# Attention with memory and two feed-forward layers on one core: attention groups reordered, weights converted in place, the first two blocks taken in two sweeps

## The chip, the cores and the metric

One core of a Trainium2 chip. The metric is the device time of one execution in microseconds (us), the median of several runs.

## The reference

```python
# B, H, S, D = 4, 8, 576, 64; all inputs float32 or float64 as drawn
scores = scale * q @ k^T, causal, softmax      # local attention
local  = a @ v
q_p    = phi(q)                                # phi(x) = where(x > 0, x, exp(x) - 1) + 1
mem    = (q_p @ M_prev) / (q_p @ z_prev + 1e-6)
g      = sigmoid(beta) per head
x      = g * mem + (1 - g) * local             # 2304 tokens x 512
x      = leaky(x @ w_in, 0.01) @ w_out         # first layer, d_ff = 2048
y      = (h - tanh(h)) @ w2_out, h = x @ w2_in # second layer, d_ff = 2048
```

The weights come as float64 and are used to a precision above one float32r product: each is split into a high and a low part, and so is each activation.

## The kernel before

**Two phases.** In the first, attention and the first layer run side by side, and the weights of both layers are turned from float64 to float32. In the second (from line 975 on) the second layer runs alone, with an order written out by hand; the change does not touch it.

**Attention** is cut into 32 units: four batches, for each a group A (queries 0 to 255, keys 0 to 255) and a group B (queries 256 to 575, all keys), for each group four pairs of heads. `Unit.declare` (L405) lists a unit's work: loads (L423 to L454), phi of q and its denominators on ScalarE and VectorE (L465 to L499), scores on TensorE (L538), maximum, exponential and sum (L571 to L607), scaling of the exponentials by 1/sum and by 1 - g (`pscale`, L609), transposes (L645, L664), the value products (L683, L686) and the copy of the result to a tile `x` (`fin`, L699). There is one x tile for the A groups and one for the B groups (`xA`, `xB`). The last 64 queries of each B group go to a ninth block R by way of DRAM.

**The first layer** takes nine blocks of 256 tokens (`layer1`, L801): the eight groups in the order A0, B0, A1, B1, ..., and R. A block's x is split into a high and a low part (`x_hi`, `x_lo`, L817 to L829; one buffer `xs`), then eight steps p follow, one for each pair of 128-column tiles of the hidden width. A step p (here an *item*) is 24 up matmuls (L794), the leak, a copy to the high part `gh`, the subtraction for the low part `gl`, and 24 down matmuls (L878). The leak is a copy from PSUM on ScalarE (`leak_a`, L848, run by the helper at L372) and a VectorE operation (`leak_b`, L853). The sums stay in PSUM (`dn0`, `dn1`) over all eight steps and are then copied out and stored (L892 to L902).

**The weights**: `convert` (L714) loads a chunk of 256 columns of a tile as integer words into a ring of four `cvr`, makes float32 words of it in a ring of four `cv` (one ScalarE operation and four VectorE operations, L731 to L747), and for the first layer writes the high part (`w_hi`, L760) and the low part (`w_lo`, L763) to the weight tile. There are 64 chunks for each layer; those of the second layer are stored to DRAM and loaded again in phase two.

**The order of the work** on each engine comes from a planner, `Schedule.run` (L144). Every piece of work has its engines with an estimated duration on each, what it reads, writes and allocates, and a due time `prio`. The planner plays the program through: whenever an engine is free, it takes the ready piece with the smallest due time that has room in its rings (`room`, L130) and emits it. On the chip each engine then runs its pieces in this order. Attention units have due times 0 to 31 with small offsets (`OFFSET`, L220), conversions of the first layer `W1_FROM + i * W1_STEP` (L225, L914), those of the second layer come behind given units, and matmuls of the first layer have the due time class `MOE_PE`, so that TensorE takes them when attention has nothing ready. `BIAS` (L224) weighs the engines where a piece can go to several. All loads and stores are issued by SP.

```python
groups = [("A", 0), ("B", 0), ("A", 1), ("B", 1), ("A", 2), ("B", 2), ("A", 3), ("B", 3)]
BIAS = {"act": 1.25, "dve": 2.5, "pool": 0.9}
W1_FROM, W1_STEP = 0, 0.15
chunks = [(m, f, c) for p in range(NP) for m in range(2) for f in (2 * p, 2 * p + 1) for c in range(512 // CW)]
```

Of the kernel before, what the change touches and what calls it, by code (L numbers as in the profile page):

```python
# [19 lines left out]
TINY = 2.0 ** -15  # L20
# [38 lines left out]
def POOL(n):  # L59
    return 160 + 0.83 * n  # L60


def POOL_S(n):
    return 328 + 0.83 * n


def POOL_TT(n):
    return 165 + 2.07 * n
# [12 lines left out]
class Op:  # L81
    __slots__ = (
        "alts", "fn", "prio", "lat", "alloc", "deps", "users", "left", "tiles", "end", "engine", "idx")


class Schedule:
# [15 lines left out]
    def op(self, alts, fn, reads=(), writes=(), alloc=(), prio=(0,), lat=0.0, after=(), war=False, order=False):  # L102
        o = Op()
        o.alts, o.fn, o.prio, o.lat, o.alloc = dict(alts), fn, prio, lat, tuple(alloc)
# [39 lines left out]
    def run(self):  # L144
# [13 lines left out]
        cold = 0.0  # L158
        events = [1000.0]
        t = -1.0  # L160
        while todo:
# [6 lines left out]
            while again:  # L168
                again = False
                for e in engines:  # L170
                    if free[e] > t:
                        continue
                    for i, (_, _, at, o) in enumerate(ready[e]):
                        if at > t or not self.room(o, t):
                            continue
# [19 lines left out]
                    o.engine, o.end = e, mine  # L195
                    free[e] = mine
# [27 lines left out]
BIAS = {"act": 1.25, "dve": 2.5, "pool": 0.9}  # L224
W1_FROM, W1_STEP = 0, 0.15  # L225
# [4 lines left out]
def kernel(  # L230
# [42 lines left out]
    mask = const.tile([128, 640], BF16, name="mask")  # L273
# [9 lines left out]
    with tc.tile_pool(name="id0", bufs=1) as id_p:  # L283
# [10 lines left out]
        out=mask[:, 512:640], in_=mask[:, 512:640], pattern=[[-1, 128]], compare_op=ALU.is_ge,  # L294
        fill=-8.0e9, base=0, channel_multiplier=1,
    )
    nc.vector.tensor_copy(out=mask4[:, 0:512], in_=mask[:, 0:512])
    for i in range(2):
        nc.vector.tensor_copy(out=mask4[64 * i:64 * i + 64, 512:S], in_=mask[0:64, 512:S])
# [9 lines left out]
    nc.vector.tensor_scalar(out=omg, in0=gate, scalar1=-1.0, scalar2=1.0, op0=ALU.mult, op1=ALU.add)  # L309
    for i in range(2):  # L310
# [4 lines left out]
    wt = [[wts.tile([128, 1024], F32R, name=f"w{m}_{f}") for f in range(NF)] for m in range(2)]  # L315
# [4 lines left out]
    def w_load(raw, a, m, f, c):  # L320
        if m == 0:
            src = a[c * CW:(c + 1) * CW, f * 128:(f + 1) * 128].bitcast(I32)
            nc.sync.dma_start(
                out=raw.rearrange("p (k c) -> p k c", k=CW // 128),
                in_=src.rearrange("(k p) c -> p k c", p=128))
        else:
            nc.sync.dma_start(
                out=raw, in_=a[f * 128:(f + 1) * 128, c * CW:(c + 1) * CW].bitcast(I32))
# [5 lines left out]
    groups = [("A", 0), ("B", 0), ("A", 1), ("B", 1), ("A", 2), ("B", 2), ("A", 3), ("B", 3)]  # L334
# [12 lines left out]
    x2s = [dram.tile([128, KT, 256], F32, name=f"x2s{n}") for n in range(NBLK)]  # L347
    x8s = dram.tile([128, KT, 256], F32, name="x8s")
# [3 lines left out]
    x_p = p1.enter_context(tc.tile_pool(name="x", bufs=1))  # L352
# [12 lines left out]
    w_h = [[[sc.new(None) for _ in range(512 // CW)] for f in range(NF)] for m in range(2)]  # L365
    v_h = [[sc.new(None) for f in range(NF)] for m in range(2)]
    x8_h = sc.new(None)
    x2_h = [sc.new(None) for n in range(NBLK)]

# [20 lines left out]
    class Unit:  # L390
# [14 lines left out]
        def declare(self, pr, prev):  # L405
# [40 lines left out]
            def load_v(e):  # L446
                v_.tile = att.tile([128, 5, 2, 64], F32, name="v", bufs=RINGS["v"])
                for i, h in enumerate(heads):
                    nc.sync.dma_start(
                        out=v_.tile[:, 0:nk, i, :],  # L450
                        in_=v[b, h, 0:nk * 128, :].rearrange("(t p) d -> p t d", p=128))
# [12 lines left out]

            def phi_exp(e):  # L465
                ph.tile = att.tile([128, 3, 2, 64], F32, name="ph", bufs=RINGS["ph"])
                nc.scalar.activation(out=flat(ph.tile), in_=flat(rq.tile), func=AF.Exp)

            def phi_line(e):
# [3 lines left out]
            def phi_min(e):  # L473
                nc.vector.tensor_tensor(out=flat(ph.tile), in0=flat(ph.tile), in1=flat(rq.tile), op=ALU.min)
# [25 lines left out]
            op([("act", ACT(nf))], phi_exp, reads=[rq], alloc=[ph])  # L500
            op([("dve", DVE(nf / 2))], phi_line, reads=[rq], writes=[rq], war=True)
            op([("dve", DVE(nf))], phi_min, reads=[rq, ph], writes=[ph])
            op([("dve", 2 * nq * 145)], phi_den, reads=[ph, zb], writes=[rq], alloc=[dn])
            op([("dve", 110)], den_inv, reads=[dn], writes=[dn])
# [16 lines left out]
            op(copies(nqc, True), p_out, reads=[s], writes=[pT])  # L521
# [41 lines left out]
            for i in range(nq):  # L563
# [7 lines left out]
                def maxi(e, j, t=t, ss=ss, ei=ei, mx=mx, nn=nn, half=half, c0=c0):  # L571
                    if t < 4:
                        out, in0, in1 = ei.tile[:, j, :], ss[j].tile[:, c0:c0 + nn], mask[:, 640 - nn:640]
# [14 lines left out]
                for j in range(2):  # L588
                    op([("dve", DVE(width))], lambda e, j=j, f=maxi: f(e, j),
# [11 lines left out]
                def sum_eps(e, t=t, sm=sm):  # L601
                    x = sm.tile[:, 0:2 if t < 4 else 1]
                    nc.vector.tensor_scalar(out=x, in0=x, scalar1=1e-9, scalar2=None, op0=ALU.add)
# [5 lines left out]
                def pscale(e, j, t=t, ei=ei, sm=sm):  # L609
                    x = ei.tile[:, j, :] if t < 4 else ei.tile[:, 0:S]  # L610
                    g = omg[:, 2 * hp + j:2 * hp + j + 1] if t < 4 else omg4[:, hp:hp + 1]
                    (nc.vector if e == "dve" else nc.gpsimd).tensor_scalar(  # L612
                        out=x, in0=x, scalar1=sm.tile[:, j:j + 1], scalar2=g, op0=ALU.mult, op1=ALU.mult)
# [6 lines left out]
                op([("dve", 85)], sum_inv, reads=[sm], writes=[sm])  # L620
                for j in both:
                    op([("pool", POOL_S(nn)), ("dve", DVE(0.83 * nn))], lambda e, j=j, f=pscale: f(e, j),
# [13 lines left out]
            for kt in range(nk):  # L636
# [42 lines left out]
                for j in range(len(ss)):  # L679
                    op(copies(2 * w if len(ss) == 1 else w, True), lambda e, j=j, f=e_out: f(e, j),  # L680
                       reads=[ss[j]], writes=[pt])

            def pv(e):  # L683
                for kt, c0, w, pt, at in parts:
                    for j in range(2):
                        nc.tensor.matmul(  # L686
                            o.tile[64 * j:64 * j + 64, c0:c0 + w], lhsT=v_.tile[:, kt, j, :],
# [7 lines left out]
            if first_x:  # L695
                x_h[key] = new("x" + kind)
            xh = x_h[key]

            def fin(e):  # L699
                if xh.tile is None:  # L700
                    xh.tile = x_p.tile([128, KT, nqc], F32, name="x" + kind)
                copy(e, xh.tile[:, hp, 0:nqc], o.tile[:, 0:nqc])

            op(copies(nqc, True), fin, reads=[o], writes=[xh], alloc=[xh] if first_x else [])
# [9 lines left out]
    def convert(m, f, c, layer, pr, after=()):  # L714
        a = ((w1_in, w1_out), (w2_in, w2_out))[layer][m]
        raw, g = sc.new("cvr"), sc.new("cv")
        op = lambda *a, **kw: sc.op(*a, prio=pr, **kw)

        def load(e):
            raw.tile = cv_p.tile([128, 2 * CW], I32, name="cvr", bufs=RINGS["cvr"])  # L720
            w_load(raw.tile, a, m, f, c)
# [3 lines left out]

        def gi():
            return g.tile.bitcast(I32)

        def c_abs(e):
            g.tile = cv_p.tile([128, CW], F32, name="cv", bufs=RINGS["cv"])  # L730
            nc.scalar.activation(out=g.tile, in_=words(1).bitcast(F32), func=AF.Abs)  # L731

        def c_max(e):
            nc.vector.tensor_scalar(out=g.tile, in0=g.tile, scalar1=TINY, scalar2=None, op0=ALU.max)  # L734
# [17 lines left out]
        op([("act", ACT(CW))], c_abs, reads=[raw], alloc=[g])  # L752
        op([("dve", DVE(CW / 2))], c_max, reads=[g], writes=[g])
# [360 lines left out]
```

## Time and profile before

| | us |
|---|---|
| median of 3 runs | 1130.25 |
| lowest, highest | 1127.24, 1130.68 |
| the profiled execution | 1126.48 |
| its span, first to last instruction | 1124.8 |
| TensorE busy in the span | 1049.4 (93%) |
| VectorE busy | 750.9 (67%) |
| ScalarE busy | 584.1 (52%) |
| GpSimd busy | 422.0 (38%) |

PE is TensorE's matmuls, PEld its weight loads, which overlap them; DVE is VectorE, ACT ScalarE, POOL GpSimd, SP the engine that issues the transfers. L794 is line 794 of the kernel. Busy shares in slices are in tenths of the slice; PEclk is the granted clock of TensorE in tenths of full speed, or as a fraction in a table by stage. A busy DVE or POOL instruction can hold time in which it was kept waiting. The span lies 1.7 us under the execution's own time.

### The profile page before, as it was taken

How to read it: one execution, taken by the hardware profiler on the slowest of the kernel's cores; microseconds unless marked ns; L12 is line 12 of the kernel's file. 1: busy time of each engine (PE TensorE's matmuls, PEld its weight loads, DVE VectorE, ACT ScalarE, POOL GpSimd, SP SyncE). 2: the span in 40 equal slices, each digit the busy share in tenths (PEclk: the TensorE clock that was granted, in tenths of full speed). 3: DMA queues.
4: the chain of work that ended last, by engine and by line, in shares of the span. 5: the costliest groups of instructions: out<-in, count | busy, mean ns of one | idle time of the engine just before them, and what ended most of it. 6: DMA issues, size and time to landing. Idle time of an engine off the chain costs nothing.

```text
span 1124.8 us, 20884 instructions
## 1 busy us (share of the span) xinstructions
PE 1049.4 (93%) x7488; PEld 915.8 (81%) x7488; DVE 750.9 (67%) x2015; ACT 584.1 (52%) x1285; POOL 422.0 (38%) x462
## 2 busy tenths in 40 slices
PE   4468889999999999999999999899999999999997
PEld 2246677779688797797999999899999999999996
DVE  8999998676973956926111115577777777777774
ACT  4556555554643635515111122576666676676664
POOL 4556555334342343343333358622222222222221
PEclk8679999999999999999999999999999999999999
DMA  6545453444742744605110014501001011010000
GB/s 190 166 136 156 124 161 77 112 112 129 211 130 59 210 130 131 187 16 161 58 38 1 20 38 145 156 2 38 9 30 39 1 38 39 1 39 19 1 20 20
DMA packets 115192, 94.17 MB, mean 84 GB/s; under 512 B 64144, under 2 KB 92816, under 8 KB 115088
## 3 DMA queue, kind: packets, MB, share of 16 engines
q1 hardware_dynamic: 115088, 92.84, 27.9%
q8 instruction: 59, 0.97, 0.3%
q14 instruction: 45, 0.37, 0.1%
HBM read 74.45 MB, written 18.35 MB: 83 GB/s over the span
## 4 chain that ended last, share of the span: by engine, by line
PE 66%; DVE 19%; DMA 5%; POOL 3%; issue 3%; ACT 2%; SPq 1%; ACTq 0%; POOLq 0%; DVEq 0%
PE up L794 30%; PE dn L1031 17%; PE dn L878 12%; DVE cv L742 3%; DVE e L577 2%; DVE cv L747 2%; PE s L664 2%; DVE cv L734 2%; PE s L551 2%; DVE rq L480 2%; DMA cvr<-in_moe_w_in_dram 2%; PE o L686 1%; DVE cv L737 1%; DVE g L853 1%; DVE e L612 1%
## 5 line engine op out<-in xcount | busy, mean ns | idle before, releaser
L794 PE MATMUL up<-xs,w 128*128 128x256 f32 x3456 | 446.7, 282 | 0.0
L794 PEld LDWEIGHTS up<-xs,w 128*128 128x128 f32 x3456 | 427.9, 190 | 11.7 <-issue 6.0
L385 POOL TENSOR_TENSOR gl<-gf,gh 128x512 fp32r<-128x512 f32 x72 | 93.6, 1300 | 301.3 <-ACT gh L1018 301.3
L878 PE MATMUL dn<-gh,w 128*128 128x256 f32 x1152 | 162.2, 288 | 3.1 <-POOL gh L331 1.7
L878 PEld LDWEIGHTS dn<-gh,w 128*128 128x128 f32 x1152 | 147.2, 193 | 9.8 <-issue 4.7
L853 DVE SCALAR_TENSOR_TENSOR g<-up,g 128x512 f32<-128x512 f32 x72 | 49.5, 687 | 156.5 <-ACT g L372 156.2
L1031 PE MATMUL dn<-w,gh 128*128 128x512 f32 x576 | 144.2, 392 | 3.2 <-ACT gh L1018 3.2
L1008 DVE SCALAR_TENSOR_TENSOR gf<-u,w 128x512 f32<-128x512 f32 x72 | 86.3, 1199 | 82.9 <-ACT w L1005 82.9
L612 POOL TENSOR_SCALAR e<-e,sm,omg 128x512 f32<-128x512 f32 (+4 forms) x85 | 76.5, 903 | 121.8 <-DVE sm L607 42.0
L1031 PEld LDWEIGHTS dn<-w,gh 128*128 128x128 f32 x576 | 103.0, 188 | 22.6 <-ACT gh L1018 3.8
L372 ACT ACTIVATE g<-up 128x512 f32<-128x512 f32 x72 | 42.6, 592 | 143.0 <-PE up L794 129.8
L597 ACT ACTIVATE e<-e,mx 128x128 f32<-128x128 f32 (+4 forms) x144 | 82.8, 577 | 49.4 <-DVE mx L577 47.4
L331 POOL TENSOR_SCALAR gh<-g 128x512 fp32r<-128x512 f32 x64 | 43.5, 680 | 170.8 <-DVE g L853 165.3
L1000 ACT ACTIVATE u<-up 128x512 f32<-128x512 f32 x72 | 43.0, 597 | 115.8 <-PE up L794 115.8
L664 PE MATMUL s<-identr,e 128*128 128x128 f32 x448 | 70.0, 293 | 26.7 <-POOL e L612 19.3
L385 POOL TENSOR_TENSOR gl<-g,gh 128x512 fp32r<-128x512 f32 x66 | 86.6, 1313 | 4.9 <-ACT gh L372 0.2
L664 PEld LDWEIGHTS s<-identr,e 128*128 128x128 f32 x448 | 52.2, 148 | 39.9 <-POOL e L612 24.6
L878 PE MATMUL dn<-gl,w 128*128 128x256 f32 x576 | 83.4, 286 | 0.0
L372 ACT ACTIVATE pt<-s 128x320 f32<-128x320 f32 (+4 forms) x159 | 62.1, 438 | 31.1 <-PE s L664 23.0
L1031 PE MATMUL dn<-w,gl 128*128 128x512 f32 x288 | 77.0, 389 | 0.0
L878 PEld LDWEIGHTS dn<-gl,w 128*128 128x128 f32 x576 | 75.1, 193 | 2.2 <-issue 2.1
L731 ACT ACTIVATE cv<-cvr 128x256 f32<-128x256 f32 x128 | 54.4, 434 | 30.6 <-DMA cvr<-in_moe_w_out_dram 13.8
(90 smaller groups left out, 1526.3 us busy)
## 6 DMA issues: line engine op xcount, KB each, us to landing
cvr<-in_moe_w_in_dram SPq DMA_DIRECT2D x64, 256.0 KB, 3.1
cvr<-in_moe_w_out_dram SPq DMA_DIRECT2D x64, 256.0 KB, 3.1
vs<-cv SPq DMA_DIRECT2D x64, 128.0 KB, 2.3
v<-vs SPq DMA_DIRECT2D x32, 256.0 KB, 2.8
qk<-in_qkt_dram SPq DMA_DIRECT2D x16, 448.0 KB, 4.2
v<-in_v_dram SPq DMA_DIRECT2D x32, 160.0 KB, 3.1
x2s<-g SPq DMA_DIRECT2D x18, 256.0 KB, 2.5
x2i<-x2s SPq DMA_DIRECT2D x9, 512.0 KB, 3.6
```

The costliest lines, as they stand in the source:

```text
L331: nc.gpsimd.tensor_scalar(out=out, in0=in_, scalar1=1.0, scalar2=0.0, op0=ALU.mult, op1=ALU.add)
L372: nc.scalar.activation(out=out, in_=in_, func=AF.Copy)
L385: (nc.vector if e == "dve" else nc.gpsimd).tensor_tensor(out=out, in0=in_, in1=high, op=ALU.subtract)
L597: nc.scalar.activation(out=x, in_=x, func=AF.Exp, scale=-1.0, bias=mx.tile[:, k:k + 1], accum_out=sm.tile[:, j:j + 1])
L612: (nc.vector if e == "dve" else nc.gpsimd).tensor_scalar(out=x, in0=x, scalar1=sm.tile[:, j:j + 1], scalar2=g, op0=ALU.mult, op1=ALU.mult)
L664: nc.tensor.transpose(ss[j].tile[:, a:a + 128], x, ident)
L731: nc.scalar.activation(out=g.tile, in_=words(1).bitcast(F32), func=AF.Abs)
L794: nc.tensor.matmul(ps()[:, s, :], lhsT=w[:, wh * 512 + kt * 128:wh * 512 + (kt + 1) * 128], rhs=xs()[:, xh, kt, :], start=(kt == 0 and j = ...
L853: nc.vector.scalar_tensor_tensor(out=g.tile, in0=ps.tile.rearrange("p a b -> p (a b)"), scalar=0.01, in1=g.tile, op0=ALU.mult, op1=ALU.max)
L878: nc.tensor.matmul(dn[m // 2].tile[:, m % 2, :], lhsT=w[:, wh * 512 + m * 128:wh * 512 + (m + 1) * 128], rhs=gg.tile[:, s * 256:(s + 1) * ...
L1008: nc.vector.scalar_tensor_tensor(out=g, in0=u, scalar=lin, in1=w, op0=ALU.mult, op1=ALU.add)
L1031: nc.tensor.matmul(dn[t], lhsT=g[:, c0:c0 + 128], rhs=w[:, wh * 512:(wh + 1) * 512], start=(p == 0 and s == 0 and j == 0), stop=(p == NP - ...
```

## The change

The edits:

- The attention groups run in the order A0, A1, A2, A3, B0, B1, B2, B3, and the blocks with them. One ring of two x tiles serves all groups.
- Blocks 0 and 1 pass the first layer in two sweeps, p 0 to 3 of block 0, then of block 1, then p 4 to 7 of block 0, then of block 1. The sums of the first sweep go to DRAM (`xps`), are loaded again and added on VectorE. Each sweep splits its x anew.
- A weight tile of the first layer is loaded whole as integer words into its own buffer, converted 512 words at a time with `cv` as the only intermediate, and its high and low parts are written over the words. At most five tiles are under way. The due times are 3.2 + 0.02 i for the first 16 tiles and 7.2 + 0.02 i for the other 16. In the second layer's conversion raw words and results share the ring `cv`.
- The planner holds GpSimd apart from the VectorE pieces not marked `port=False`: only one of the two runs at a time. Its estimates and weights change.
- The leak is one ScalarE operation, Prelu. Phi is Relu and Exp on ScalarE and one VectorE operation. 1 - g goes into the sum's reciprocal, and the scaling of the exponentials has one factor and may run on ScalarE too.
- The values of a B unit come in one load; a mask is shorter.

```diff
-    "qk": 2, "rq": 1, "zb": 2, "mb": 2, "v": 1, "ph": 1, "dnm": 2, "pT": 1, "mx": 6, "sm": 6,
-    "e2": 1, "e3": 1, "e4": 1, "s": 3, "o": 1, "pt": 4, "xA": 1, "xB": 1, "xs": 1,
-    "g": 2, "gl": 2, "gh": 2, "up": 2, "dn0": 1, "dn1": 1, "cvr": 4, "cv": 4, "v2": 4,
+    "qk": 2, "rq": 1, "zb": 2, "mb": 2, "v": 2, "ph": 1, "dnm": 2, "pT": 1, "mx": 6, "sm": 6,
+    "e2": 1, "e3": 1, "e4": 1, "s": 3, "o": 1, "pt": 4, "x": 2, "xs": 1,
+    "g": 2, "gl": 2, "gh": 2, "up": 2, "dn0": 1, "dn1": 1, "cv": 4, "v2": 4,
...
-                        if at > t or not self.room(o, t):
+                        shared = e == "pool" or (e == "dve" and o.port)
+                        if at > t or (shared and port_free > t) or not self.room(o, t):
...
+                    if e == "pool" or (e == "dve" and o.port):
+                        port_free = mine
...
-BIAS = {"act": 1.25, "dve": 2.5, "pool": 0.9}
-W1_FROM, W1_STEP = 0, 0.15
+AHEAD = 5
+BIAS = {"act": 1.0, "dve": 1.5, "pool": 1.1}
+W1_FROM, W1_STEP = (3.2, 7.2), 0.02
+SPLIT = 2
...
-    groups = [("A", 0), ("B", 0), ("A", 1), ("B", 1), ("A", 2), ("B", 2), ("A", 3), ("B", 3)]
+    groups = [(k, b) for k in "AB" for b in range(B)]
...
+    SWEEPS = [(n, h * NP // 2, (h + 1) * NP // 2) for h in range(2) for n in range(SPLIT)]
+    SWEEPS += [(n, 0, NP) for n in range(SPLIT, NBLK)]
...
-                nc.scalar.activation(out=flat(ph.tile), in_=flat(rq.tile), func=AF.Exp)
-                nc.vector.tensor_scalar(
-                    out=flat(rq.tile), in0=flat(rq.tile), scalar1=1.0, scalar2=1.0, op0=ALU.add, op1=ALU.max)
-                nc.vector.tensor_tensor(out=flat(ph.tile), in0=flat(ph.tile), in1=flat(rq.tile), op=ALU.min)
+                nc.scalar.activation(out=flat(ph.tile), in_=flat(rq.tile), func=AF.Relu, scale=-1.0)
+                nc.scalar.activation(out=flat(ph.tile), in_=flat(ph.tile), func=AF.Exp, scale=-1.0)
+                nc.vector.scalar_tensor_tensor(
+                    out=flat(ph.tile), in0=flat(rq.tile), scalar=1.0, in1=flat(ph.tile), op0=ALU.add, op1=ALU.max)
...
-                    (nc.vector if e == "dve" else nc.gpsimd).tensor_scalar(
-                        out=x, in0=x, scalar1=sm.tile[:, j:j + 1], scalar2=g, op0=ALU.mult, op1=ALU.mult)
+                    r = sm.tile[:, j:j + 1]
+                    if e == "act":
+                        nc.scalar.activation(out=x, in_=x, func=AF.Copy, scale=r)
+                    elif e == "dve":
+                        nc.vector.tensor_scalar(out=x, in0=x, scalar1=r, scalar2=None, op0=ALU.mult)
+                    else:
+                        nc.gpsimd.tensor_scalar(
+                            out=x, in0=x, scalar1=r, scalar2=0.0, op0=ALU.mult, op1=ALU.add)
...
-        raw, g = sc.new("cvr"), sc.new("cv")
+        n = 512 if layer == 0 else CW
+        raw, g = sc.new(None if layer == 0 else "cv"), sc.new("cv")
...
+            if layer == 0:
+                raw.tile = wts.tile([128, 1024], I32, name=f"w{m}_{f}")
+            else:
+                raw.tile = cv_p.tile([128, 2 * CW], I32, name="cv", bufs=RINGS["cv"])
+            w_load(raw.tile, a, m, f, c, n)
...
-            op([("act", ACT(CW)), ("pool", POOL(CW))], w_hi, reads=[g], writes=[wh])
-            op(lows(CW), w_lo, reads=[g, wh], writes=[wh])
+            op(copies(512), w_hi, reads=[g], writes=[wh])
+            op(lows(512), w_lo, reads=[g, wh], writes=[wh])
...
-            def leak_b(e, ps=ps, g=g):
-                nc.vector.scalar_tensor_tensor(
-                    out=g.tile, in0=ps.tile.rearrange("p a b -> p (a b)"), scalar=0.01, in1=g.tile,
-                    op0=ALU.mult, op1=ALU.max)
+            def leak(e, ps=ps, g=g):
+                g.tile = g_p.tile([128, 512], F32, name="g")
+                nc.scalar.activation(
+                    out=g.tile, in_=ps.tile.rearrange("p a b -> p (a b)"), func=AF.Prelu, alpha=0.01)
...
+            if p0 > 0:
+                sop([("sp", 500)], part_load, reads=[xp_h[n][i]], alloc=[x2], after=[last], lat=2300)
+                sop([("dve", DVE(512))], x2_out, reads=[dn[i], x2], writes=[x2], port=False)
+            else:
+                sop(copies(512, True), x2_out, reads=[dn[i]], alloc=[x2], port=False)
...
-    for i, (m, f, c) in enumerate(chunks):
-        convert(m, f, c, 0, (0, W1_FROM + i * W1_STEP))
+    firsts = []
+    for i, (m, f) in enumerate((m, f) for p in range(NP) for m in range(2) for f in (2 * p, 2 * p + 1)):
+        firsts.append(convert(m, f, 0, 0, (0, W1_FROM[i // (2 * NP)] + i * W1_STEP), firsts[i - AHEAD:i - AHEAD + 1] if i >= AHEAD else ()))
...
-    for n in range(NBLK):
-        layer1(n)
+    for sweep in SWEEPS:
+        layer1(*sweep)
```

## Rows read from the trace of the kernel before

**Rows 1.** The page, the span in 40 slices of 28.1 us.
```profile
PE   4468889999999999999999999899999999999997
DVE  8999998676973956926111115577777777777774
PEclk8679999999999999999999999999999999999999
```

**Rows 2.** Table by stage: window us, length, busy us of each engine, PEclk, DMA share, GB/s.
```profile
core 0: us, PE busy (x) PEld busy (x) DVE busy (x) ACT busy (x) POOL busy (x), PEclk, DMA share, GB/s
0.00:84.00 84.00, 45.74 (x184) 25.16 (x186) 79.43 (x300) 43.93 (x129) 43.74 (x71) 0.74 0.58 165
84.00:168.00 84.00, 72.20 (x523) 56.92 (x519) 83.89 (x287) 47.85 (x139) 49.39 (x68) 0.96 0.50 148
168.00:560.00 392.00, 377.58 (x2921) 317.02 (x2920) 259.45 (x1014) 185.88 (x502) 150.93 (x171) 1.00 0.43 124
560.00:700.00 140.00, 139.26 (x1156) 138.65 (x1156) 30.45 (x39) 26.69 (x46) 64.72 (x65) 1.00 0.13 43
730.00:1100.00 370.00, 370.00 (x2404) 337.13 (x2403) 272.88 (x345) 254.06 (x427) 87.14 (x67) 1.00 0.06 21
```

**Rows 3.** The chain of waits, two dense runs of 24 (start us, us).
```profile
333.12 2.88 PE dn L878 x24
336.00 2.88 PE up L794 x24
```

**Rows 4.** Line L794 alone (up matmuls), table by stage.
```profile
0.00:168.00 168.00, 24.87 (x168) 21.73 (x168) 0.85 0.54 156
168.00:560.00 392.00, 129.64 (x936) 117.85 (x937) 1.00 0.43 124
```

**Rows 5.** Line L878 alone (down matmuls), table by stage.
```profile
0.00:168.00 168.00, 19.64 (x128) 17.68 (x128) 0.85 0.54 156
168.00:560.00 392.00, 131.75 (x953) 119.86 (x952) 1.00 0.43 124
```

**Rows 6.** Line L686 alone (value matmuls), table by stage.
```profile
0.00:168.00 168.00, 15.92 (x120) 8.84 (x120) 0.85 0.54 156
168.00:560.00 392.00, 36.89 (x328) 21.50 (x328) 1.00 0.43 124
```

**Rows 7.** Timeline of ACT: first and last x piece of A0, first split of x.
```profile
18.51 0.36 ACT L372 ACTIVATE xA<-o 128x256 f32<-128x256 f32 x1
...
64.98 0.36 ACT L372 ACTIVATE xA<-o 128x256 f32<-128x256 f32 x1
65.25 0.62 ACT L372 ACTIVATE xs<-xA 128x512 fp32r<-128x512 f32 x1
```

**Rows 8.** Timeline of DVE: first and last operation of the first attention unit.
```profile
5.42 0.29 DVE L470 TENSOR_SCALAR rq<-rq 128x256 f32<-128x256 f32 x1 [0.46 <-ACT ph L467]
...
8.60 0.72 DVE L612 TENSOR_SCALAR e<-e,sm,omg 128x128 f32<-128x128 f32 x2
```

**Rows 9.** Groups of instructions, whole run: count | busy us, mean ns | idle before.
```profile
L1008 DVE SCALAR_TENSOR_TENSOR gf<-u,w 128x512 f32<-128x512 f32 x72 | 86.3, 1199 | 82.9 <-ACT w L1005 82.9
...
L742 DVE SCALAR_TENSOR_TENSOR cv<-cvr,cv 128x256 int32<-128x256 int32 x128 | 63.2, 501 | 0.4
...
L372 ACT ACTIVATE g<-up 128x512 f32<-128x512 f32 x72 | 42.6, 592 | 143.0 <-PE up L794 129.8 <-issue 9.8 <-DVE w L385 2.8
...
L853 DVE SCALAR_TENSOR_TENSOR g<-up,g 128x512 f32<-128x512 f32 x72 | 49.5, 687 | 156.5 <-ACT g L372 156.2
...
L734 DVE TENSOR_SCALAR cv<-cv 128x256 f32<-128x256 f32 x128 | 44.5, 351 | 6.9 <-ACT cv L731 6.5
...
L612 DVE TENSOR_SCALAR e<-e,sm,omg 128x128 f32<-128x128 f32 (+4 forms) x59 | 27.8, 476 | 0.5
...
L385 DVE TENSOR_TENSOR xs<-xA,xs 128x512 fp32r<-128x512 f32 x10 | 7.3, 732 | 18.8 <-ACT xs L372 18.8
...
L306 ACT ACT_TABLE_LOAD x1 | 1.3, 1283 | 0.8 <-PEq L1099 0.8
```

**Rows 10.** DMA issues: KB each, median us to landing.
```profile
cvr<-in_moe_w_in_dram SPq DMA_DIRECT2D x64, 256.0 KB, 3.1
```

More of the change, by code (lines that the diff above doesn't have):

```diff
@@ L82 @@
     __slots__ = (
-        "alts", "fn", "prio", "lat", "alloc", "deps", "users", "left", "tiles", "end", "engine", "idx")
+        "alts", "fn", "prio", "lat", "alloc", "deps", "users", "left", "tiles", "end", "engine", "idx", "port")
 class Schedule:
@@ L100, in new, with op @@
         return Handle(tag, seq)
-    def op(self, alts, fn, reads=(), writes=(), alloc=(), prio=(0,), lat=0.0, after=(), war=False, order=False):
+    def op(self, alts, fn, reads=(), writes=(), alloc=(), prio=(0,), lat=0.0, after=(), war=False, order=False, port=True):
         o = Op()
+        o.port = port
         o.alts, o.fn, o.prio, o.lat, o.alloc = dict(alts), fn, prio, lat, tuple(alloc)
@@ L364 @@
     x_h = {}
-    w_h = [[[sc.new(None) for _ in range(512 // CW)] for f in range(NF)] for m in range(2)]
+    w_h = [[sc.new(None) for f in range(NF)] for m in range(2)]
     v_h = [[sc.new(None) for f in range(NF)] for m in range(2)]
@@ L368 @@
     x2_h = [sc.new(None) for n in range(NBLK)]
+    xp_h = [[sc.new(None) for i in range(2)] for n in range(NBLK)]
+    SWEEPS = [(n, h * NP // 2, (h + 1) * NP // 2) for h in range(2) for n in range(SPLIT)]
+    SWEEPS += [(n, 0, NP) for n in range(SPLIT, NBLK)]
+    seqs = [0]
     def copy(e, out, in_):
@@ L619, in declare @@
                 op([("dve", 70)], sum_eps, reads=[sm], writes=[sm])
-                op([("dve", 85)], sum_inv, reads=[sm], writes=[sm])
+                op([("dve", 85)], sum_inv, reads=[sm], writes=[sm], port=False)
                 for j in both:
-                    op([("pool", POOL_S(nn)), ("dve", DVE(0.83 * nn))], lambda e, j=j, f=pscale: f(e, j),
+                    op([("act", ACT(nn)), ("pool", POOL_S(nn)), ("dve", DVE(nn / 2))], lambda e, j=j, f=pscale: f(e, j),
                        reads=[sm], writes=[ei])
@@ L695, in declare @@
             if first_x:
-                x_h[key] = new("x" + kind)
+                x_h[key] = new("x")
             xh = x_h[key]
@@ L831, in layer1 @@
         last = None
-        for p in range(NP):
-            seq = n * NP + p
+        for p in range(p0, p1):
+            seq = seqs[0]
+            seqs[0] += 1
             ps = sc.new("up")
@@ L863, in g_lo @@
                 low(e, gl.tile, g.tile, gh.tile.bitcast(F32))
-            sop([("act", ACT(512, True))], leak_a, reads=[ps], alloc=[g])
-            sop([("dve", DVE(512))], leak_b, reads=[ps, g], writes=[g])
+            sop([("act", ACT(512, True))], leak, reads=[ps], alloc=[g])
             sop(copies(512), g_hi, reads=[g], alloc=[gh])
-            sop(lows(512), g_lo, reads=[g, gh], alloc=[gl])
+            last = sop(lows(512), g_lo, reads=[g, gh], alloc=[gl])
             for j, (wh, gg) in enumerate(((0, gh), (1, gh), (0, gl))):
```

154 lines of the change are left out of this document (84 added, 70 removed).

## The prediction

> **What bounds the kernel now.** I read the page's slices first [rows 1]: TensorE (PE) is at 9 tenths from slice 7 to the end, but at 4 to 8 in slices 0 to 6, where VectorE (DVE) is at 9 nearly throughout and the clock row falls to 6 and 7. The table by stage puts numbers to it [rows 2]: up to 84 us PE is busy 45.7 us at a mean granted clock of 0.74, from 84 to 168 us 72.2 us, and from 168 to 560 us 377.6 of 392 us at full clock; after that nothing is left to gain (139.3 of 140, 370 of 370). DVE is busy 79.4 and 83.9 us in the two stretches of 84. So the kernel is bound by PE except at its start, and there by DVE.
>
> How much is lost at the start? A layer-one item (one block, one p) is 24 up and 24 down matmuls, 2.88 us each when dense [rows 3]: 5.76 us, 0.12 us a matmul. By 168 us there were 168 of the first kind and 128 of the second [rows 4, 5], worth 35.5 us. From 168 to 560 us there were 936 + 953, worth 226.7 us, so that of the 377.6 us busy 150.9 went to attention, with 328 of the 448 value matmuls [rows 6]. I scale attention by these: 0.46 us each, 120 before 168 us, 55.2 us. A unit A has 8 of them (3.7 us), a unit B 20 (9.2 us). The first 168 us hold 90.7 us of full-speed PE work: **77 us are lost** to waiting and to the low clock.
>
> The cause is the order. The four units of A0 end at 18.5 to 65.0 us, some 15.5 us apart, and only then can layer one split its first input [rows 7]: 64 weight conversions at due times 0 to 9.5 run among them, all on DVE, and B0's heavier units come next.
>
> **The change part by part.**
>
> *Order, two sweeps.* Units A0 to A3 come first; conversions start at due time 3.2, behind A0; blocks 0 and 1 run p 0 to 3 as soon as half the weights are there. I look for T, the time from which PE has layer-one work without a break: A0 and A1 done, 16 of the 32 weight tiles converted.
>
> VectorE to T. The first unit ran nearly alone: its DVE work, all but one scaling, lies between 5.42 and 9.32 us, gaps included, 3.9 us [rows 8]; eight units, 31 us. A conversion of 512 words is two one-input operations (0.40 each: the present 0.351 for 256 words, grown less than in proportion, since an operation has a fixed part) and two of two inputs; a two-input operation on 512 measures 0.732 [rows 9]. With the low half on DVE too (0.732) that is 3.0 us, for 16 tiles 48 us; with it on GpSimd (POOL), 36 us and 16 POOL operations. Together with 5 us before the first work: 5 + 31 + 48 = 84 us, less what POOL and ScalarE (ACT) take. Lower bound 72 us (POOL has the low halves); upper bound 105 us, if waits between the engines hold DVE up by a quarter (PE stands idle 14% of the second stretch and 46% of the first). I take **T = 85 us**.
>
> ScalarE to T. ACT is busy 91.7 us in 168 us [rows 2] for eight units, part of a ninth and all 64 half tiles. To T there is half the weights and only A units: at most 46 us. Added: a second pass over phi (about 0.4 us a unit, 3 us), the weights' high halves now mostly here (about 10 us), scaling of the exponentials (four a unit, some 0.35 us: 11 us). 70 us: less than DVE, but close.
>
> Work in PE up to T: four items (23 us) and eight A units (29 us), 52 us; lost 85 - 52 = 33 us. From T to 168 us there is layer-one work, but DVE still converts 16 tiles (48 us) and serves A2 and A3 (31 us). Idle in such a mix is between 3.7% (14.4 of 392 us, 168 to 560) and 14% (84 to 168) [rows 2]; I take the near row, 14% of 83 us, 12 us. Lost in all 45 instead of 77 us: **gain 32 us**.
>
> *Prelu.* One ACT operation replaces the copy (592 ns) and the DVE operation (687 ns, 72 times, 49.5 us) [rows 9]. It reads 512 words of PSUM as the copy does, so ACT keeps its time; DVE has idle time wherever most items run. Ending the detour through DVE shortens the way from up to down, which two items' lag covers. Nothing, save in the first stage, where four to a dozen items give DVE 3 to 8 us: inside T's bounds.
>
> *Phi, one-scalar scaling, 512-wide conversion.* DVE gives up a 0.4 us operation per unit, and gets the scaling (0.476 us on DVE now) with one operand less; already in the 3.9 us as an upper bound. After 168 us they cost or bring nothing: PE is the bound there.
>
> *The exclusion in the planner.* It changes order alone. The wait is in today's durations already: the same DVE operation on 512 words takes 687 ns with an input from PSUM, and 1199 ns in phase two with both in SBUF beside a working POOL [rows 9]. No gain of its own; it is why I use uncrowded durations to T.
>
> *Transfers.* To T 8 MB of weights and eight units' inputs, some 5 MB: 13 MB in 80 us, 165 GB/s, which is what the first 84 us move at a DMA share of 0.58 [rows 2]. Hidden by DVE; if the loads were late, T would move with them. On SP's queue 32 weight loads and 16 value loads fall away, four stores and four loads of partial sums come in. The loads wait for their sweep's last low half and are queued ahead of attention's loads, which run two units ahead; at 3 us a load [rows 10] that costs nothing while PE has blocks in store.
>
> *Second sweep.* Two more splits of x and two more evacuations: PE covers them with the downs of the item before, as at today's eight block changes. The adds read PSUM on DVE, 0.7 us each. Nothing; uncovered, about 2 us each, 4 us.
>
> *Layer-two conversions.* Raw data and result share one ring of four, taken in turn: two chunks under way instead of four. A chunk is a load (3.1 us), five operations of about 0.5 and a store, 8 us; 64 of them at two a time need 256 us, and from A3's third unit, before 168 us, to the end of attention, near 560, there are some 400. Nothing.
>
> *Back pressure.* Two x buffers stay two: attention runs at most two blocks ahead, so B units alternate with dense layer-one work. Idle after 168 us stays as it is (14 us); 8 us either way.
>
> Sum against the profiled execution: 1126.5 - 32 = 1094.5 us. The median of the runs shown is 1130.25, 3.8 us above it; I forecast the median, **1098 us**. Its own range is T from 75 to 105 us: lost 36 to 62 us, 1089 to 1115 us.
>
> **The rivals.**
>
> *More (0.13).* ACT and POOL take enough from DVE for T near 72 us, and from T on the idle share is 3.7%: lost 20 + 4 = 24 us, and the planner's truer model halves the 14 us after 168: gain about 60, 1070 us. For it: DVE's inflated durations. Against it: work in chains rarely packs that tightly; PE waited for POOL and ACT too.
>
> *Less (0.15).* The bound passes to chains across engines and T is 105 to 118 us: gain 15 down to 4 us, 1115 to 1126 us. For it: ACT's 70 us are close to DVE's 84, and weights, phi and scaling all moved there.
>
> *Nothing (0.06).* T = 118 to 126, or the gain is given back by B units run back to back: starved PE after 168 us. Against that: B units in the trace need PE 9.2 us each, and layer one has two blocks (92 us) in store.
>
> *Slower: ScalarE switches tables (0.08).* One ACT_TABLE_LOAD of 1283 ns stands in the trace [rows 9], ahead of all activations; Prelu is not among the functions that ran on it. If it needs another table, each item in the attention stage brings two loads, 2.57 us. To T that is 4 items, 10 us on ACT, which then is level with DVE. Up to 560 us 42 more items: 108 us on an engine with 186 us busy and some 65 moved to it, 359 of 392 us, as full as DVE is at 84 to 168 us, where PE idles 14%. That would be 55 instead of 14 us: 1094.5 + 10 + 41 = 1146 us. It decides if more than half the items need a load; with fewer, ACT stays below 80% and the gain stands.
> The Trainium skill ("ScalarE: Activation LUTs", Table sets: the hidden batching unit) has a rule that speaks against the change here: functions in different sets cost a load at each switch, and it names relu, abs and tanh beside exp, but not Prelu. By that rule alone the time would be the 1146 us; the trace agrees so far as its functions share one load.
>
> **How the numbers follow.** The forecast's own case has 0.58. Over 0.3% (3.4 us, about what a measurement of this kernel can tell) faster are it, "more" and "less": 0.86; same 0.06; slower 0.08. The range 1076 to 1126 us leaves out half of "more", the slower case and half of "nothing": 0.18.
>
> **What would show it.** The four units of A0 end within about 35 us; the first split of x by 40 us; PE at 9 tenths from about slice 3; the clock row at 9 from there; some 500 layer-one matmuls by 168 us instead of 296; DVE full only to about 150 us; one table load. Wrong if ACT rather than DVE is full before T, if PE has gaps after 168 us with x ready, or if the first split is still at 60 us.

## The result, and the profile after

The changed kernel takes 1095.2 us (median of 4 runs, 1094.44 to 1096.48), the kernel before 1129.3 us; the ratio is 0.9701, interval 0.9681 to 0.972. That is 34 us less; 1098 us and a gain of 32 us were forecast. The profiled execution has a span of 1093.1 us against 1124.8.

The page's slices of the kernel after, 27.3 us each, to be set beside [rows 1]:

```profile
PE   4796999999999999999999999999999999999997
...
DVE  6999977878658748845222156777777777777774
ACT  5868576767547638635111023776667666676664
POOL 0000000000000000000000000122222222222221
PEclk8597899999999999999999999999999999999999
```

PE is at 9 tenths in slice 2 (counted from 0) and from slice 4 on; before, from slice 7 on. Slices 0, 1 and 3 hold most of what is lost, and the clock row has its 5 and 7 right there. The POOL row is at nothing up to slice 24, the end of phase one; before, GpSimd was busy 244 us up to 560 us [rows 2: 43.7 + 49.4 + 150.9]. The table by stage (window, length, busy us of PE, PEld, DVE, ACT, POOL, granted clock, DMA share, GB/s), beside [rows 2]:

```profile
56.00:84.00 28.00, 27.62 (x216) 26.38 (x215) 26.34 (x86) 19.30 (x42) 0.74 (x2) 0.94 0.47 151
84.00:112.00 28.00, 18.12 (x83) 11.38 (x84) 27.66 (x101) 22.66 (x62) 0.00 (x0) 0.73 0.74 221
112.00:140.00 28.00, 28.00 (x212) 27.31 (x210) 26.14 (x70) 17.70 (x36) 0.00 (x0) 0.90 0.06 16
140.00:168.00 28.00, 28.00 (x229) 23.05 (x228) 22.25 (x126) 20.35 (x66) 0.00 (x0) 1.00 0.46 115
...
168.00:560.00 392.00, 387.44 (x2989) 323.11 (x2988) 259.94 (x1001) 220.94 (x539) 4.48 (x18) 1.00 0.45 129
...
670.00:730.00 60.00, 59.86 (x430) 56.37 (x429) 46.22 (x67) 38.26 (x64) 9.30 (x8) 1.00 0.25 79
```

PE works from 56 to 84 us, has a hole from 84 to 112 us, where it is busy 18.1 of 28 us at a clock of 0.73, and is full from then on; from 168 to 560 us it idles 4.6 us, where it idled 14.4. The passage to phase two in the kernel before, for the last line:

```profile
670.00:730.00 60.00, 56.69 (x461) 55.77 (x460) 27.71 (x34) 24.20 (x41) 46.68 (x45) 1.00 0.51 158
```

The up, down and value matmuls alone, in the same two stretches as [rows 4 to 6]:

```profile
0.00:168.00 168.00, 40.57 (x271) 37.99 (x272) 0.82 0.55 163
168.00:560.00 392.00, 129.59 (x955) 119.44 (x953) 1.00 0.45 129
```

```profile
0.00:168.00 168.00, 32.15 (x240) 29.79 (x240) 0.82 0.55 163
168.00:560.00 392.00, 131.40 (x946) 119.39 (x947) 1.00 0.45 129
```

```profile
0.00:168.00 168.00, 15.06 (x104) 7.64 (x104) 0.82 0.55 163
168.00:560.00 392.00, 39.03 (x344) 23.03 (x344) 1.00 0.45 129
```

By the prediction's own reckoning: 271 + 240 layer-one matmuls by 168 us at 0.12 us are 61.3 us (before 35.5). From 168 to 560 us the 955 + 946 are worth 228.1 of 387.4 us, which leaves 159.3 us for 344 value matmuls; the 104 before 168 us then stand for 48.2 us. That is 109.5 us of full-speed work in 168 us, and 58.5 us lost instead of 77. So the start gave about **18.5 us**, the stretch from 168 to 560 us **9.9 us**, and the passage to phase two **3.2 us** (PE idle 3.3 us from 670 to 730 us before, 0.1 us after): 31.6 of the span's 31.7 us. The share of attention is an estimate, scaled by its value matmuls. Without it: all 448 of them are done by 560 us in both kernels, and 227 more layer-one matmuls are, worth 27.2 us; less the 9.9 us, that leaves 17.4 us for the start.

The x pieces and splits on ACT, beside [rows 7]:

```profile
22.63 0.36 ACT L393 ACTIVATE x<-o 128x256 f32<-128x256 f32 x1
...
50.21 0.36 ACT L393 ACTIVATE x<-o 128x256 f32<-128x256 f32 x1
50.47 0.62 ACT L393 ACTIVATE xs<-x 128x512 fp32r<-128x512 f32 x1
...
81.20 0.38 ACT L393 ACTIVATE x<-o 128x256 f32<-128x256 f32 x1 [0.20 <-PE o L717]
...
104.90 0.63 ACT L393 ACTIVATE xs<-x 128x512 fp32r<-128x512 f32 x1
```

A0's last piece is written at 50.2 us (before 65.0), A1's first piece at 81.2 us, and A1's input is split at 104.9 us. Four items of block 0 ran between.

### The profile page after: what moved, and what is told of

Read it like the earlier page. It is cut to its first block, busy times and chain, and to the rows that moved or that the text cites. A ratio compares the mean times of both kernels' runs of the same rounds, so it can differ in the third digit from the quotient of the medians.

```text
span 1093.1 us, 20334 instructions
## 1 busy us (share of the span) xinstructions
PE 1047.4 (96%) x7488; PEld 920.1 (84%) x7488; DVE 753.0 (69%) x2029; ACT 640.0 (59%) x1348; POOL 101.1 (9%) x103
## 4 chain that ended last, share of the span: by engine, by line
PE 81%; DVE 7%; DMA 4%; ACT 4%; issue 1%; SPq 1%; ACTq 0%; DVEq 0%
PE up L835 34%; PE dn L1081 18%; PE dn L915 16%; PE s L695 4%; PE o L717 3%; PE s L576 3%; DMA w<-in_moe_w_out_dram 2%; DMA cv<-in_moe_w_in_dram 1%; PE o L662 1%; ACT e L622 1%; PE s L581 1%; DVE e L602 1%; DVE cv L786 1%; DVE w L406 1%; DVE cv L781 1%
## 5 line engine op out<-in xcount | busy, mean ns | idle before, releaser
L395 DVE CAST gh<-g 128x512 fp32r<-128x512 f32 x39 | 16.7, 427 | 106.0 <-ACT g L892 105.9
L602 DVE CUSTOM_DVE_ANT_0 e<-s,mask 128x128 f32<-128x128 f32 (+4 forms) x144 | 64.0, 483 | 11.3 <-PE s L576 10.3
L393 ACT ACTIVATE pt<-s 128x320 f32<-128x320 f32 (+4 forms) x148 | 57.9, 437 | 18.9 <-PE s L683 12.8
L1081 PEld LDWEIGHTS dn<-w,gl 128*128 128x128 f32 x288 | 54.1, 188 | 11.2
L576 PE MATMUL s<-qk 64*128 64x128 f32 (+3 forms) x256 | 56.0, 524 | 5.3 <-DMA qk<-in_qkt_dram 4.5
L1061 DVE COPY_PREDICATED gf<-mk,up 128x512 f32<-128x512 int32 x72 | 53.7, 746 | 7.8 <-DVE up L1060 0.5
```

Source lines behind the costliest of these rows:

```text
L393: nc.scalar.activation(out=out, in_=in_, func=AF.Copy)
L576: nc.tensor.matmul(ss[j].tile[:, c0:c0 + nn], lhsT=qk.tile[p, a:a + 128], rhs=qk.tile[p, kc:kc + nn], start=True, stop=True)
L602: nc.vector.tensor_tensor_reduce(out=out, in0=in0, in1=in1, scale=-scale, scalar=mx.tile[:, 0:1] if t == 4 and j else BIG, op0=ALU.add, op ...
L1061: nc.vector.copy_predicated(out=g, mask=mk.bitcast(I32), data=h)
L1081: nc.tensor.matmul(dn[t], lhsT=g[:, c0:c0 + 128], rhs=w[:, wh * 512:(wh + 1) * 512], start=(p == 0 and s == 0 and j == 0), stop=(p == NP - ...
```

## The experiments

Ratios are to the kernel before, run on the same chip beside each; the changed kernel has 0.9701.

**1. The exclusion taken out.**

```diff
-                        shared = e == "pool" or (e == "dve" and o.port)
+                        shared = False
```

> The changed kernel, but the planner lets GpSimd and VectorE run side by side again (all else as changed). Theory 1 (the exclusion is order only, the time comes from the order of groups and weights): within 5 us of 1095, 1090 to 1100 us, with GpSimd busy again by some 100 us or more up to 168 us. Rival (the exclusion takes GpSimd out of the chain of attention, and the 10 us of TensorE idle time that went between 168 and 560 us went by that): 1103 to 1110 us, with TensorE idle above 12 us from 168 to 560 us.

Measured: 1118.5 us, ratio 0.9894 (0.9873 to 0.9915). Two thirds of the gain are gone, more than the rival had it; POOL is busy only 32 us up to 168 us, not 100, so the little work it has must cost much. That stretch, and the longest wait of PE in it (engine, line, waited for: us, times, longest):

```profile
0.00:168.00 168.00, 117.43 (x758) 93.14 (x759) 141.89 (x503) 103.18 (x265) 31.96 (x28) 0.80 0.52 156
```

```profile
PE s L695 <- POOL e L643: 16.1, 2, 8.2
```

Two waits of 16.1 us in all, for two scalings on POOL. The run's three scalings on POOL, and DVE's timeline during the first of them (start us, us, engine, line):

```profile
51.75 6.96 POOL L643 TENSOR_SCALAR e<-e,sm 128x256 f32<-128x256 f32 x1 [12.09 <-DVE sm L633]
...
116.26 6.62 POOL L643 TENSOR_SCALAR e<-e,sm 128x256 f32<-128x256 f32 x1 [9.70 <-DVE sm L633]
...
237.16 0.59 POOL L643 TENSOR_SCALAR e<-e,sm 128x384 f32<-128x384 f32 x1 [21.22 <-DVE sm L633]
```

```profile
51.48 0.67 DVE L781 SCALAR_TENSOR_TENSOR cv<-w,cv 128x512 int32<-128x512 int32 x1
52.06 0.68 DVE L406 TENSOR_TENSOR w<-cv,w 128x512 fp32r<-128x512 f32 x1
...
57.35 0.41 DVE L773 TENSOR_SCALAR cv<-cv 128x512 f32<-128x512 f32 x1
57.69 0.68 DVE L781 SCALAR_TENSOR_TENSOR cv<-w,cv 128x512 int32<-128x512 int32 x1
61.69 0.69 DVE L406 TENSOR_TENSOR w<-cv,w 128x512 fp32r<-128x512 f32 x1 [3.32 <-ACT w L393]
```

The third scaling, of 384 words, took 0.59 us; the first, of 256 words, started at 51.75 us and ended at 58.71: DVE runs its conversions without a gap, none of them longer than usual (0.68 and 0.41 us), and POOL is done 0.34 us after the last of them, when DVE stands idle. DVE loses nothing; POOL gets no turn for 14 operations of DVE. Between 168 and 560 us PE idles 7.7 us here and 4.6 in the changed kernel: the loss is at the start, and some 5 us in the passage to phase two.

**2. One sweep.** `SPLIT = 2` becomes `SPLIT = 0`.

> The changed kernel with each block in one pass, p 0 to 7, no partial sums. Theory 1 (the sweeps let TensorE go on with block 1 while the second half of the weights is converted): 1103 to 1112 us, TensorE waits for weights behind block 0's p 3. Rival (in the changed kernel TensorE stood idle from 84 to 112 us for want of block 1's input while 9 tiles of the second half were ready, so that one pass would have had work there): 1088 to 1097 us.

Measured: 1095.09 us, ratio 0.9697 (0.968 to 0.9714). The sweeps bring nothing that can be told from zero; the rival holds. With one pass PE is busier in the hole (22.4 of 28 us from 84 to 112 us) and less so behind it (19.0 of 28 us from 112 to 140 us, 28.0 in the changed kernel).

**3. The old order of groups.**

```diff
-    groups = [(k, b) for k in "AB" for b in range(B)]
+    groups = [(k, b) for b in range(B) for k in "AB"]
```

> The changed kernel with the groups and blocks in the order A0, B0, A1, B1 again, the two sweeps then over A0 and B0. Theory 1 (A groups first bring the second input early, at four light units): the second x comes some 25 us later, 1108 to 1120 us. Rival (VectorE is full in either order and the order only moves the hole): 1093 to 1100 us.

Measured: 1101.76 us, ratio 0.9752 (0.9732 to 0.9773), 6.6 us slower than the changed kernel and 28 us faster than the one before: between the two expectations. The order is worth a fifth of the gain at most (see experiment 12).

**4. The second half of the weights held back.**

```diff
-..., firsts[i - AHEAD:i - AHEAD + 1] if i >= AHEAD else ()))
+..., (firsts[i - AHEAD:i - AHEAD + 1] if i >= AHEAD else []) + ([ends[7]] if i >= 2 * NP else [])))
```

> The changed kernel, and the second 16 weight tiles begin only when A1's last unit has been written out. Theory 1 (VectorE is the bound until the second input is there, and in the changed kernel it converted 9 tiles, 26 us, ahead of need): block 1's input is split near 85 to 90 us instead of 105, TensorE's hole from 84 to 112 us closes, 1080 to 1089 us. Rival (A1's units are held by their own chain of engines and transfers, and the tiles only filled gaps): the split stays near 100 us, the weights come later, 1096 to 1110 us.

Measured: 1098.36 us, ratio 0.9723 (0.9701 to 0.9745). The split moved from 104.9 to 102.1 us only. The split, and the stretch of the hole in this run:

```profile
102.06 0.61 ACT L393 ACTIVATE xs<-x 128x512 fp32r<-128x512 f32 x1
```

```profile
84.00:112.00 28.00, 21.34 (x116) 13.22 (x115) 17.70 (x88) 17.51 (x49) 0.00 (x0) 0.76 0.62 185
```

DVE is busy 17.7 of 28 us, ACT 17.5, and the hole is still there: in it A1's units were not held by VectorE's load, and the nine tiles had only filled gaps. Theory 1 falls. That it is the units' own chain, as the rival has it, is argued; no run shows the link that sets their pace.

**5. The exclusion alone, in the kernel before** (the added `port` of the pieces and the one condition, nothing else).

> The kernel before, and nothing changed but the planner's exclusion of GpSimd and VectorE (estimates, weights and order as before). Theory 1 (keeping the two engines apart is the change's main part and works in either kernel): 1100 to 1115 us. Rival (it matters in the changed kernel alone, where an operation of GpSimd meets long runs of VectorE operations on 512 words; in the kernel before GpSimd's longest scaling took 1.9 us): 1124 to 1140 us.

Measured: 1128.11 us, ratio 0.9985 (0.9964 to 1.0006). No difference: the rival holds. POOL keeps its work there, 272 us up to 560 us (244 before), so this run does not show what an empty POOL would do in the kernel before: with the new engine weights besides, it was not run.

**6. No exclusion, scalings off POOL.** As experiment 1, and

```diff
-op([("act", ACT(nn)), ("pool", POOL_S(nn)), ("dve", DVE(nn / 2))], ...
+op([("act", ACT(nn)), ("dve", DVE(nn / 2))], ...
```

> The changed kernel without the exclusion, like e1_no_exclusion, but the scaling of the exponentials may not go to GpSimd (its other pieces may). In e1_no_exclusion two scalings of 256 words took 6.96 and 6.62 us there, and TensorE waited 16 us for them. Theory 2 (the 23 us of the exclusion are starved operations of GpSimd in the chain of attention): most of it comes back, 1098 to 1106 us. Rival (they come from VectorE and GpSimd slowing each other all over): 1112 to 1119 us.

Measured: 1110.55 us, ratio 0.9829 (0.9802 to 0.9856). A third of the loss comes back, between theory and rival. Part of the rest has the same form: POOL now had low halves of g in layer one's way, and two were starved; PE waited 3.8 us for one. Of the 16 us by which this span is longer than the changed kernel's, though, 7 lie behind 168 us (PE idle 7.2 us up to 560 us, 4.6 us from 670 to 730 us), and what costs them is not shown. The two, with DVE's timeline around the end of the longer:

```profile
64.39 5.09 POOL L406 TENSOR_TENSOR gl<-g,gh 128x512 fp32r<-128x512 f32 x1 [11.08 <-DMA w<-in_moe_w_in_dram]
...
121.52 10.06 POOL L406 TENSOR_TENSOR gl<-g,gh 128x512 fp32r<-128x512 f32 x1 [17.60 <-DVE cv L776]
```

```profile
130.04 0.43 DVE L776 TENSOR_SCALAR cv<-cv 128x512 int32<-128x512 int32 x1
130.38 0.29 DVE L602 CUSTOM_DVE_ANT_0 e<-s,mask 128x128 f32<-128x128 f32 x1
130.59 0.09 DVE L602 DVE_READ_ACCUMULATOR2_ANT mx<- 128x1 f32 x1
130.59 1.55 DVE L781 SCALAR_TENSOR_TENSOR cv<-w,cv 128x512 int32<-128x512 int32 x1
132.06 0.68 DVE L406 TENSOR_TENSOR w<-cv,w 128x512 fp32r<-128x512 f32 x1
```

10.06 us, where 1.30 is the rule in phase two. POOL got its turn when DVE came to an operation that reads PSUM (130.38, the maximum): the next DVE operation took 1.55 us instead of 0.68, now kept waiting itself, and POOL ended at 131.58.

**7. Two buffers for q, one for the values.** `"rq": 1` becomes 2, `"v": 2` becomes 1.

> The changed kernel with two buffers for q instead of one, and one for the values instead of two (there is no room for both). Theory 3 (an attention unit of A0 and A1 takes 8 us because its q is loaded only when the unit before has done with the buffer: load, phi, denominators in a row): the second split comes 10 us or more before 105 us, 1083 to 1091 us. Rival (the units' pace is VectorE's work): 1093 to 1098 us.

Measured: 1093.57 us, ratio 0.9682 (0.9654 to 0.9711), not to be told from the changed kernel. The second split is at 106.9 us. Theory 3 falls, though the run makes two edits: the single buffer of the values could have taken something back, but PE waited for values only once in A1's units, 1.6 us. What sets their pace of 8 us stays open. This run's first 168 us:

```profile
0.00:168.00 168.00, 137.08 (x876) 109.20 (x878) 149.38 (x572) 114.88 (x301) 2.31 (x12) 0.97 0.56 164
```

The granted clock is 0.97 here and 0.82 in the changed kernel, yet PE is still busy only 19.2 us from 84 to 112 us, and the span is not shorter (1095.2 against 1093.1 us). So the low clock at the start is not the main thing that costs time there.

**8. The old leak** in the changed kernel (copy on ScalarE and `scalar_tensor_tensor` on VectorE, `port=False`).

> The changed kernel with the leak as before, a copy on ScalarE and an operation on VectorE. The prediction's step (Prelu is worth nothing but some us in the first stage): 1094 to 1099 us. Rival (the shorter way from up to down is what took TensorE's idle time from 14 to 5 us between 168 and 560 us): 1102 to 1108 us.

Measured: 1107.17 us, ratio 0.9795 (0.9766 to 0.9824), 12 us slower by the medians, 11 by the ratios. Block 1's split comes at 113.5 us instead of 104.9; PE idles 8.5 us from 168 to 560 us instead of 4.6, and 2.5 us from 670 to 730 us instead of 0.1. The rival named a part of it; most is at the start.

**9. Nothing for POOL, no exclusion.** As experiment 6, and copies and low halves without their POOL alternative.

> The changed kernel without the exclusion, and with nothing of the first phase but small fills for GpSimd (copies, low halves and scalings go to ScalarE or VectorE). Theory 2 (the exclusion pays because it leaves GpSimd without work; 7 to 10 us starts of single GpSimd operations beside VectorE were its whole cost): as the changed kernel, 1091 to 1099 us. Rival (keeping the two apart has a worth beyond that): 1104 to 1120 us.

Measured: 1098.04 us, ratio 0.9705 (0.9677 to 0.9733): the changed kernel's ratio. The exclusion has no worth beyond leaving POOL empty that this measurement could tell, and against experiment 1 the work on POOL alone costs 20 us.

**10. The exclusion, and the old engine weights.**

```diff
-BIAS = {"act": 1.0, "dve": 1.5, "pool": 1.1}
+BIAS = {"act": 1.25, "dve": 2.5, "pool": 0.9}
```

> The changed kernel, exclusion and all, with the engine weights of before (ScalarE 1.25, VectorE 2.5, GpSimd 0.9), so that GpSimd gets work again, one engine at a time. Theory 2 (work of attention on GpSimd costs, exclusion or not, as in the kernel before with the exclusion, 1128 us): 1108 to 1128 us. Rival (with the exclusion GpSimd does no harm): 1092 to 1102 us.

Measured: 1124.93 us, ratio 0.9943 (0.9925 to 0.9962). Four fifths of the gain are gone, with order, sweeps, in-place weights, Prelu and exclusion all there. Its first 168 us and the changed kernel's:

```profile
0.00:168.00 168.00, 115.10 (x685) 88.99 (x686) 135.85 (x405) 102.59 (x266) 74.28 (x70) 0.77 0.49 147
```

```profile
0.00:168.00 168.00, 134.28 (x863) 107.33 (x864) 148.79 (x567) 117.89 (x304) 2.96 (x13) 0.82 0.55 163
```

POOL has 74.3 us of work instead of 3.0, and PE is busy 115 us instead of 134. What the work on POOL takes off the others is read from the whole run, where both kernels have done the same work (this run, then the changed kernel):

```profile
PE 1052.2 (94%) x7488; PEld 920.8 (82%) x7488; DVE 665.4 (59%) x1715; ACT 661.8 (59%) x1408; POOL 362.9 (32%) x357
```

```profile
PE 1047.4 (96%) x7488; PEld 920.1 (84%) x7488; DVE 753.0 (69%) x2029; ACT 640.0 (59%) x1348; POOL 101.1 (9%) x103
```

262 us more on POOL relieve DVE of 88 us, and ACT has 22 us more. That it is the work on POOL that costs the time is argued here: all three weights change at once, and PE's longest waits up to 168 us are for ACT, and those for POOL come third:

```profile
PE o L662 <- ACT pT L393: 18.2, 5, 5.8
PE s L695 <- ACT e L639: 10.5, 9, 3.1
PE s L539 <- POOL ph L522: 10.0, 5, 3.0
```

**11. Prelu alone, in the kernel before.**

> The kernel before with the leak as one Prelu. In the changed kernel the old leak cost 12 us (1107 against 1095). Theory 4 (Prelu takes 0.69 us of VectorE and one engine change out of every item, worth as much in either kernel): 1114 to 1122 us. Rival (in the kernel before its items lie where VectorE has time; the 12 us come from a new plan in the crowded stage up to 112 us): 1126 to 1132 us.

Measured: 1133.78 us, ratio 1.0024 (1.0008 to 1.004). The rival holds, though 2 us above its range: no gain there. PE's idle time from 168 to 560 us is 16.7 us (14.4).

**12. Estimates 2 ns higher.** The constants of `DVE` and `ACT` rise from 69, 94 and 52 to 71, 96 and 54.

> The changed kernel, and the planner's estimates of VectorE and ScalarE operations 2 ns higher: no engine's work changes, only the plan. It shows how far a new plan alone moves the time. Theory 5 (the plan is robust; differences of 6 us and more between the kernels tried are their edits): 1092 to 1098 us. Rival (any new plan moves the time by 5 us and more, so that the smaller differences say little): outside 1090 to 1100 us.

Measured: 1093.14 us, ratio 0.9659 (0.9626 to 0.9693), 0.4% under the changed kernel by the ratios (0.0042 of 1129 us, 4.7 us; by the medians 2.1 us). This one new plan moved the time by 2 to 5 us; another can move it by more. So experiments 1, 6, 8 and 10 stand clear of it, experiment 3 (6 to 7 us) hardly, and experiments 2, 4, 7 and 9 say "no more than a plan".

## Why the prediction was right, and where it was wrong

The time and the size of the gain came out within 3 us, but by a sum whose terms were wrong in both directions. That they cancel is luck.

**What bounds the kernel: right in the main.** More than half of the gain came from the start, and PE was full behind it. DVE was full up to about 140 us, as forecast, and ACT was not the bound. But a full DVE is not always one that others wait for: from 84 to 112 us experiment 4 takes 10 us of work from it, and PE's hole stays.

**T: mis-sized.** I took 85 us from DVE's work alone. Work without a break begins at about 112 us, past even the upper bound of 105; the case "less" had this T. Each operation's price was near (two-input conversions 0.69 us, I took 0.73; one-input 0.42, I took 0.40), and the order of the work was not. A0 ended at 50.2 us, not 35: half of the 16 tiles were converted between its units. From 50 to 72 us DVE does little but convert the other half (seven tiles), and A1 waits for it: the phi of its first unit is through on ACT at 44.0 us, and DVE takes it up at 75.4.

```profile
50.00:72.00 22.00, 20.80 (x138) 19.21 (x139) 20.34 (x43) 14.10 (x26) 0.00 (x0) 0.78 0.70 230
```

```profile
43.58 0.42 ACT L495 ACTIVATE ph<-ph 128x256 f32<-128x256 f32 x1
```

```profile
75.40 0.42 DVE L498 SCALAR_TENSOR_TENSOR ph<-rq,ph 128x256 f32<-128x256 f32 x1
```

Then A1's units end 8 us apart on average (81.2 to 104.5 us), twice the 3.9 us that I took for one. Experiment 4 shows that this pace is not VectorE's load, and experiment 7 speaks against the one buffer of q; it stays open.

**The idle time behind T: forecast at 12 us, measured at nothing.** PE is busy 56 of 56 us from 112 to 168 us. Up to 112 us it did what I had put before T; the up, down and value matmuls up to then:

```profile
0.00:112.00 112.00, 15.91 (x102) 14.88 (x102) 0.75 0.70 212
```

```profile
0.00:112.00 112.00, 12.26 (x96) 11.78 (x96) 0.75 0.70 212
```

```profile
0.00:112.00 112.00, 10.71 (x64) 5.21 (x64) 0.75 0.70 212
```

By the same reckoning these are 53 us of work (I took 52), so some 59 us are lost up to T and nothing behind it, where I had 33 and 12. The start gave 18.5 us instead of 32. The sign "some 500 layer-one matmuls by 168 us" still came (511), because PE had no gaps behind T.

**After 168 us: the step "idle stays as it is", with its 8 us either way, failed.** PE's idle time fell from 14.4 to 4.6 us, and that of the passage to phase two by 3 us. These 13 us, which no step had, made up for T. What took them is not settled: up to 560 us PE idles 7.7 us without the exclusion and 8.5 us with the old leak, so neither edit alone accounts for the 9.9 us.

**The exclusion: the step "no gain of its own" failed as put, and its reason with it.** I argued that the wait is in today's durations already. But the exclusion does more than write the wait down: with the new engine weights it leaves POOL without work. And the durations of the kernel before held no wait like those of experiment 1, where an operation on POOL waits through a whole run of DVE's. Without the exclusion the kernel is 23 us slower (experiment 1), and with POOL emptied by other means nothing is lost that can be told (experiment 9); the exclusion alone, in the kernel before, is worth nothing (experiment 5). Experiment 10 shows that the weights matter as much: exclusion with the old weights has 6 of the 34 us. I had left `BIAS` without a step.

**The two sweeps: priced as part of the order, and worth nothing that can be told** (experiment 2). The order itself is worth 7 us at most (experiment 3), not the main part of 32.

**Prelu: "nothing, save in the first stage" is right for the kernel before** (experiment 11), **wrong for the changed kernel**, where the old leak costs 11 to 12 us (experiment 8). With POOL empty, DVE carries all low halves as well, and the leak's 0.69 us an item comes on top of a full engine. That it is this load, and not an unlucky plan, is argued: the plan's own share can be 5 us of the 12 or more.

**The table load: did not come.** One load stands in the trace after, and Prelu runs at the copy's price (the groups of instructions; columns as in [rows 9]):

```profile
L892 ACT ACTIVATE g<-up 128x512 f32<-128x512 f32 x72 | 42.7, 593 | 162.5 <-PE up L835 160.4 <-issue 1.8
...
L317 ACT ACT_TABLE_LOAD x1 | 1.3, 1283 | 0.8 <-PEq L1149 0.8
```

72 times 593 ns, where the copy took 592: Prelu shares the one load with the other functions that ran. The Trainium skill's rule ("ScalarE: Activation LUTs", Table sets: the hidden batching unit) charges a load for a switch between sets; the trace has no switch, so the rule charged nothing here.

**Scaling and phi, transfers, second conversion: not shown apart.** Behind 168 us they and the back pressure together cost at most the 4.6 us that PE idles up to 560 us. No run takes out the conversion of 512 words in place, its due times, phi, the scaling with one factor or the planner's new estimates, so their share of the 34 us is not known. What the runs with one edit undone lose (23, 12, 7 us) is no split of the gain: it adds up to more than 34.

## What to carry to other kernels

In this kernel GpSimd beside a full VectorE was not a spare engine: count what a piece on it takes from both, and try leaving it empty before balancing work onto it. A planner that doesn't know this must be told, or the piece must be kept off the chain that others wait for. Where a list of edits is planned as one, ask of each edit which engine it empties; here the exclusion with the old engine weights had 6 us, the new weights without it 11 us, both together 34 us, with all other edits in place each time. And run a plan that changes nothing else beside the experiments, to see which differences are too small to read.

## What the runs showed of the hardware

A GpSimd operation beside an unbroken run of VectorE operations on SBUF can wait for the whole run, not for one operation: 6.96 and 6.62 us for scalings of 256 words, where one of 384 words took 0.59 us, and 5.09 and 10.06 us for low halves, where 1.30 us is the rule, while VectorE's own, 8 to 18 of them in a row, kept their 0.41 and 0.68 us. It need not come out so: at 105.66 us of experiment 1 an operation of GpSimd took its usual 0.91 us, and VectorE's next one 1.10 us instead of 0.68. In the kernel before, with shorter operations, the longest scaling on GpSimd took 1.9 us (the view of tile e on POOL; count, shortest, median and longest ns, first and last start us, shapes):

```profile
L612 POOL TENSOR_SCALAR e<-e,sm,omg x85: 447/875/1911, 9.8 to 527.3; 128x512 f32<-128x512 f32 x21, 128x384 f32<-128x384 f32 x20, 128x256 f32<-128x256 f32 x16, 128x128 f32<-128x128 f32 x14
```

The long waits ended when VectorE went idle, or came to an operation that reads PSUM (experiments 1 and 6). The Trainium skill ("SBUF — State Buffer", SBUF: two separate sides) calls the shared pair of ports an exclusive lock that whoever starts first holds for the whole instruction. The trace agrees that one waits for the other; that the loser's wait can last for 8 to 18 instructions is shown by these runs. That it is this pair of ports for which they wait is the page's account; the runs show only who waited and for how long.
